# One bank and one evacuation for both heads of chunk 1, and the diagonal's sums in two blocks of 64 tokens

## The chip, the cores and the metric

The kernel runs on one core of one Trainium2 chip. The metric is the device time of one execution, in microseconds; lower is better. The kernel before takes 498.93 us (median of three runs, 497.51 to 500.3).

## The reference

The computation is a linear recurrence with a decaying state per batch and head, followed by a feed-forward layer with a PReLU between its two products. There are 4 batches, 8 heads, 768 tokens and 48 numbers per head; the layer goes from 384 to 2048 and back.

```python
for t in range(S):
    cur = np.einsum('bhd,bhe->bhde', u[None] * kt, vt)
    y[:, :, t] = np.einsum('bhd,bhde->bhe', rt, state + cur)
    state = w[None, :, :, None] * state + np.einsum('bhd,bhe->bhde', kt, vt)
...
h = x @ w_in                       # x: y as (3072, 384)
g = np.maximum(h, 0.0) + alpha * np.minimum(h, 0.0)
return (g @ w_out).astype(np.float32)
```

All of it is in fp32. The layer's products are made from pairs of fp32r numbers, a high part and the remainder: each product is hi*hi + lo*hi + hi*lo, three matmuls.

## The kernel before

**Chunks, pairs, steps.** The 768 tokens are cut into 6 chunks of 128, and the 8 heads into 4 pairs q. A pair keeps one head (g = 0) on partitions 0 to 47 and the other (g = 1) on partitions 64 to 111. The recurrence is done by chunk in matrix form: scores within the chunk (r times k, masked), the same token's own term on the diagonal (u), and the state carried from chunk to chunk. From chunk 1 on, a chunk is worked as two halves of 64 tokens (j = 0, 1).

The layer is worked in steps (c, i): chunk c and the i-th of 16 blocks of w_in and w_out. `m_in` (L628) makes a 128 x 512 block of h out of nine matmuls, ACT and DVE turn it into the pair gh, gl (L636 to L641), and `m_out` (L661) adds nine more to three accumulators. Steps 0 to 8 belong to chunk 0, steps 9 to 17 to chunk 1, and only then come the other 7 blocks for both chunks. For each block, its raw weights are loaded (L308, two buffers) and split by two operations on ACT and four on DVE (L326 to L337); the four have means of 0.55, 1.05, 1.00 and 0.98 us, 3.6 us of DVE a block; this must be done for blocks 0 to 8 in steps 0 to 8.

**Diagonal.** For chunks 0 and 1, `diagonal` (L466) gets the diagonal from TensorE: DVE multiplies r by k (`prod`, L468), four fp32 matmuls (one per batch, L473) multiply it by u/w (`uw`, 2 columns), and ACT copies the sums to `cu` (L477). An fp32 matmul leaves two records in the trace, so a diagonal has 8. `first_chunk` (L389) calls it once per pair, `prepare` (L485) once per pair of chunk 1. Later chunks take it from POOL.

**Chunk 0.** `first_chunk` scales r and k (L399), makes the diagonal, the scores (L410), the masked score matrix `base` (L417 on ACT, L421 on DVE), multiplies it by v (L431), and splits the result y into xh and xl with `splits` (L354): a copy on ACT (L361) and a subtraction on DVE (L362). For three pairs one operation each of 112 partitions x 512 does both heads; for the last pair there is one of 48 x 512 for each head.

**Later chunks.** `burst` (L524) does on PE the output of a pair whose `prepare` is done (`before`) and the products of the next one (`now`). The output of the pair `before` is summed in two banks, y[0] and y[1]: `through_state` (16 matmuls, L569), `through_scores(0)` (8, L579), and, after ACT has read two numbers of y[1] (`seen_y`, L592), `through_scores(1)` (8, L579). All these matmuls use a quarter of the array: rows 0 to 63 or 64 to 127 and columns 0 to 63 or 64 to 127. `where` puts head g into bank y[g], its batches 0 and 1 on its own half of the partitions and 2 and 3 on the other half:

```python
o = g ^ (b >> 1)
return y[g]()[half(o), (b & 1) * L + j * HI:(b & 1) * L + (j + 1) * HI]
```

Through the state, head g multiplies from rows half(g); so in each bank only one half of the array's rows writes at a time, and all four quarters are used. The products of the pair `now` (L543, L550) are laid out in the same way, in banks A[0] and A[1]; DVE takes them up with L598 and L605. The evacuation of a pair is four `splits` of 48 x 256 (two per head).

**Where the heads go.** Pair 0 goes to tiles of its own (`top`); pair q > 0 goes to block k = q - 1 of x. The rows 48 to 63 and 112 to 127 of that block are filled by `lower` (L344) with pieces of pair 0, by DMAs of 32 KB on SP's queue (L350). Parts 0 and 1 of a block are these rows, parts 2 to 5 the heads' rows. The first `m_in` of a chunk needs all of its x.

**The order.** Nothing is ordered by the hardware alone: `Plan.in_order` simulates the engines with the cost that each `add` states and a rank, and so writes the order of every engine's instructions, SP's queue among them. Five PSUM banks are handed out by it one at a time (`psum()`), to whoever is next: a diagonal's sums in chunk 1, y, A and the blocks of h. A burst takes its banks when it starts. Before the first step, gaps of the plan on PE are filled with small matmuls (`warm`, L721, counted by `fill`).

Of the kernel before, what the change touches and what calls it, by code (L numbers as in the profile page):

```python
# [18 lines left out]
L = 128  # L19
# [4 lines left out]
HI = 64  # L24
# [152 lines left out]
def rwkv_prelu_kernel(ctx: ExitStack, tc, rk, vkr, wP, uP, u, wall, alpha, w, r_all, k_all, v_all, oT):  # L177
# [288 lines left out]
    def diagonal(q, r, k0, cu, sums, cols, mine, prod_rank, sum_rank, copy_rank):  # L466
        prod = sb([112, B, L], "g", 3)
        add("DVE", 0.7, lambda: nc.vector.tensor_tensor(out=prod(), in0=r(), in1=k0(), op=ALU.mult),  # L468
            r=[r, k0], w=[prod], rank=prod_rank)

        def c_sum():
            for b in range(B):
                nc.tensor.matmul(sums()[:, cols][:, 2 * b:2 * b + 2], prod()[:, b], uw()[:, q], start=True,  # L473
                                 stop=True, skip_group_check=True)

        add("PE", 1.0, c_sum, r=[prod, uw], w=[mine], rank=sum_rank)
        add("ACT", 0.2, lambda: nc.scalar.activation(  # L477
            cu(), sums()[:, cols].rearrange("p (b g) -> p g b", g=2), AF.Copy), r=[mine], w=[cu], rank=copy_rank)
# [45 lines left out]
    def burst(i, was, at):  # L524
# [28 lines left out]
        if before:  # L553
            (c0, q0), r0, v0, base0, *states0 = before
            y = [psum() for _ in range(2)]
            uses += [r0, v0, base0, *states0]
            spare = psum()
            writes += y

            def where(g, b, j):  # L560
                o = g ^ (b >> 1)
                return y[g]()[half(o), (b & 1) * L + j * HI:(b & 1) * L + (j + 1) * HI]

            def through_state():
                for j, t in enumerate(states0):
                    for e in range(2):
                        for g in range(2):
                            for b in (e, e + 2):
                                nc.tensor.matmul(where(g, b, j), t()[half(g), b],  # L569
                                                 r0()[half(g), b, HI * j:HI * (j + 1)], start=(j == 0 and e == 0),  # L570
                                                 stop=False, skip_group_check=True)
# [18 lines left out]
        if before:  # L590

            seen = add("ACT", 0.2, lambda: nc.scalar.activation(seen_y(), y[1]()[0:1, L + HI - 1:L + HI + 1], AF.Copy),  # L592
                       r=[y[1]], rank=at - 200)
            seen.soon[first] = 0.75
            add("PE", 0.3, lambda: through_scores(1), r=[v0, base0], w=y, rank=at - 200)
        if now:
# [13 lines left out]
        if before:  # L610
            h, l, kx = x_tiles(c0, q0)
            for g in (1, 0):
                for o in (g, 1 - g):
# [286 lines left out]
```

## Time and profile before

| what | us |
|---|---|
| median of three runs | 498.93 |
| the profiled execution, device time | 498.5 |
| its span, first to last instruction | 496.7 |
| PE busy (x4563) | 477.7 |
| DVE busy (x550) | 322.1 |
| ACT busy (x565) | 242.5 |
| mean granted TensorE clock | 0.987 |

A busy TensorE (PE) means that matmul records cover the time. The share of each engine over the whole span is an average over two stages that differ, so the views below are by stretch.

### The profile page before, as it was taken

Reading aid. Unit: us, or ns where it says so; the run is one execution under the profiler, and the core shown is the slowest. Engines: PE = TensorE matmul, PEld = TensorE weight load, DVE = VectorE, ACT = ScalarE, POOL = GpSimd, SP = SyncE. Lnnn points to the kernel's source line nnn. Section 1 sums busy time; section 2 is a strip of 40 time slices with the busy share of each in tenths; the row PEclk is TensorE's granted clock in tenths of the full one; section 3 lists DMA queues with packets and bytes.
Section 4 is the critical chain, followed back from the end, with each engine's and each line's share of the span. In section 5 each row is a group of like instructions: output and inputs, shape, how many; then the busy total and the mean of one; then the engine's idle time right before and its main releaser. Section 6 shows DMA issues by size and latency. Waiting matters only on the chain.

```text
span 496.7 us, 11103 instructions
## 1 busy us (share of the span) xinstructions
PE 477.7 (96%) x4563; PEld 390.2 (79%) x4563; DVE 322.1 (65%) x550; ACT 242.5 (49%) x565; POOL 45.1 (9%) x49
## 2 busy tenths in 40 slices
PE   7989878999999999999999999999999999999994
PEld 6857756788888888888888888888888878888883
DVE  7799999999986677656647546747535434333331
ACT  3777557666764455535535635535633333423332
POOL 2000100001312112100311101211000000000000
PEclk9799999999999999999999999999999999999998
DMA  7965575374152253413212213312120000100001
GB/s 220 299 172 189 153 226 196 126 233 161 49 189 90 80 169 100 147 43 83 86 36 86 95 56 84 86 36 70 63 54 1 1 1 1 64 0 2 0 1 68
DMA packets 24888, 47.39 MB, mean 95 GB/s; under 512 B 4096, under 2 KB 12416, under 8 KB 24832
## 3 DMA queue, kind: packets, MB, share of 16 engines
q1 hardware_dynamic: 24832, 46.62, 30.3%
q8 instruction: 38, 0.62, 0.5%
q14 instruction: 18, 0.15, 0.1%
HBM read 37.96 MB, written 6.29 MB: 89 GB/s over the span
## 4 chain that ended last, share of the span: by engine, by line
PE 84%; DVE 8%; ACT 3%; DMA 2%; issue 1%; SPq 0%; DVEq 0%; ACTq 0%
PE acc L661 38%; PE bank L628 36%; PE bank L569 2%; PE bank L579 2%; PE bank L550 2%; PE bank L543 2%; DMA wraw<-wall 1%; DVE wx L333 1%; DVE xl L362 1%; DMA raw<-rk 1%; DVE wl L337 1%; DVE wx L330 1%; DVE g L637 1%; PE acc L473 1%; DVE raw L496 1%
## 5 line engine op out<-in xcount | busy, mean ns | idle before, releaser
L637 DVE SCALAR_TENSOR_TENSOR g<-bank,alph,g 128x512 f32<-128x512 f32 x96 | 72.0, 750 | 110.0 <-ACT g L636 108.5
L636 ACT ACTIVATE g<-bank 128x512 f32<-128x512 f32 x96 | 57.3, 597 | 141.0 <-PE bank L628 139.1
L628 PE MATMUL bank<-xh,wh 128*128 128x512 f32 x288 | 113.6, 395 | 3.4 <-DVE T L605 3.4
L628 PE MATMUL bank<-xh,wl 128*128 128x512 f32 x288 | 112.3, 390 | 0.4 <-DVE wl L337 0.3
L628 PE MATMUL bank<-xl,wh 128*128 128x512 f32 x288 | 112.1, 389 | 0.0
L640 ACT ACTIVATE gh<-g 128x512 fp32r<-128x512 f32 x96 | 60.6, 632 | 71.3 <-DVE g L637 71.1
L641 DVE TENSOR_TENSOR gl<-g,gh 128x512 fp32r<-128x512 f32 x96 | 70.0, 730 | 37.1 <-ACT gh L640 37.0
L661 PE MATMUL acc<-gh,wh 128*128 128x512 f32 x288 | 83.6, 397 | 1.6 <-ACT gh L640 1.6
L661 PE MATMUL acc<-gl,wh 128*128 128x512 f32 x288 | 83.2, 396 | 0.0
L661 PE MATMUL acc<-gh,wl 128*128 128x512 f32 x288 | 81.7, 391 | 0.0
L628 PEld LDWEIGHTS bank<-xh,wh 128*128 128x128 f32 x288 | 54.1, 188 | 15.8 <-ACT wx L326 3.8
L628 PEld LDWEIGHTS bank<-xh,wl 128*128 128x128 f32 x288 | 54.1, 188 | 12.6 <-DVE wl L337 1.3
L661 PEld LDWEIGHTS acc<-gl,wh 128*128 128x128 f32 x288 | 54.1, 188 | 12.1
L628 PEld LDWEIGHTS bank<-xl,wh 128*128 128x128 f32 x288 | 54.0, 188 | 11.7
L661 PEld LDWEIGHTS acc<-gh,wl 128*128 128x128 f32 x288 | 53.9, 188 | 11.6
L661 PEld LDWEIGHTS acc<-gh,wh 128*128 128x128 f32 x288 | 52.6, 188 | 13.2 <-ACT gh L640 1.9
L507 POOL TENSOR_TENSOR rr<-rr,kk 128x384 f32<-128x384 f32 x16 | 21.4, 1337 | 294.9 <-DMA kk<-vkr 155.8
L518 ACT ACTIVATE base<-ident,cu 128x64 f32<-128x64 f32 x160 | 41.4, 337 | 1.1 <-DVE cu L513 1.0
L362 DVE TENSOR_TENSOR xl<-bank,xh 48x256 fp32r<-48x256 f32 (+2 forms) x85 | 37.2, 438 | 3.5 <-ACT xh L361 1.7
L361 ACT ACTIVATE xh<-bank 48x256 fp32r<-48x256 f32 (+2 forms) x85 | 33.3, 392 | 7.8 <-PE bank L431 3.4
L496 DVE TENSOR_TENSOR raw<-raw,W 112x512 f32<-112x512 f32 x40 | 26.3, 681 | 0.3 <-DMA raw<-rk 0.3
L509 POOL TENSOR_TENSOR rr<-rr,utab 128x384 f32<-128x384 f32 x16 | 21.0, 1310 | 1.3
(93 smaller groups left out, 375.1 us busy)
## 6 DMA issues: line engine op xcount, KB each, us to landing
wraw<-wall SPq DMA_DIRECT2D x16, 768.0 KB, 4.8
raw<-rk SPq DMA_DIRECT2D x46, 224.0 KB, 4.2
v<-vkr SPq DMA_DIRECT2D x24, 192.0 KB, 4.0
kk<-vkr SPq DMA_DIRECT2D x24, 192.0 KB, 3.6
rr<-vkr SPq DMA_DIRECT2D x16, 192.0 KB, 2.4
oT<-o SPq DMA_DIRECT2D x12, 256.0 KB, 2.1
oT<-g SPq DMA_DIRECT2D x6, 256.0 KB, 2.6
xh<-xh SPq DMA_DIRECT2D x36, 32.0 KB, 2.5
```

The lines of the kernel that those rows point to most:

```text
L361: add("ACT", us, lambda: nc.scalar.activation(to(h), view(), AF.Copy), r=[src], w=refs(h), rank=rank)
L362: add("DVE", us + 0.1, lambda: nc.vector.tensor_tensor(out=to(l), in0=view(), in1=to(h), op=ALU.subtract), r=[src] + refs(h), w=refs(l), r ...
L496: add("DVE", 0.72, lambda t=t, tab=tab: nc.vector.tensor_tensor(out=t().rearrange("p b (j t) -> p (b j) t", j=2), in0=t().rearrange("p b ( ...
L507: add("POOL", 1.2, lambda: nc.gpsimd.tensor_tensor(out=rt(), in0=rt(), in1=k(), op=ALU.mult), r=[k] + ([wh[12]] if c == 2 else []), w=[rt] ...
L509: add("POOL", 1.2, lambda: nc.gpsimd.tensor_tensor(out=rt().rearrange("p (g b) e -> p g b e", g=2), in0=rt().rearrange("p (g b) e -> p g b ...
L518: add("ACT", 0.32, lambda g=g, b=b: nc.scalar.activation(base()[:, g, b], ident2(), AF.Copy, scale=cu()[:, g, b:b + 1]), r=[cu, ident2], w ...
L628: nc.tensor.matmul(hp()[:, :], a[i]()[:, k], x[c]()[:, k], start=(k == 0 and j == 0), stop=(k == NK - 1 and j == 2))
L636: add("ACT", 0.6, lambda: nc.scalar.activation(g(), hp()[:, :], AF.Copy), r=[hp], w=[g], rank=n - 100)
L637: add("DVE", 0.75, lambda: nc.vector.scalar_tensor_tensor(out=g(), in0=hp()[:, :], scalar=alph()[:, i:i + 1], in1=g(), op0=ALU.mult, op1=A ...
L640: add("ACT", 0.64, lambda: nc.scalar.activation(gh(), g(), AF.Copy), r=[g], w=[gh], rank=n - 100)
L641: add("DVE", 0.73, lambda: nc.vector.tensor_tensor(out=gl(), in0=g(), in1=gh(), op=ALU.subtract), r=[g, gh], w=[gl], rank=n - 99)
L661: nc.tensor.matmul(banks[k](), a[i]()[:, NK + k], x(), start=(begin and j == 0), stop=(end and j == 2))
```

## The change

The change has two parts. In `diagonal`, each of the four matmuls becomes two, of 64 tokens each, whose results go to partitions 0 to 63 and 64 to 127; the planner's cost of the piece goes from 1.0 to 0.5. In `burst`, when the pair `before` is of chunk 1 (`joint`), both heads' outputs go to one bank: head g on its own half of the partitions, batch b at column 128 b. Then the evacuation is one operation of 112 x 512 per engine for pairs 0 to 2, which also writes part 0 of the block (rows 48 to 63), and one of 48 x 512 per head for pair 3. A bank is taken from the planner for one y in place of two. `spare` was not used by any piece.

```diff
--- before.py
+++ after.py
@@ -470,10 +470,12 @@
 
         def c_sum():
             for b in range(B):
-                nc.tensor.matmul(sums()[:, cols][:, 2 * b:2 * b + 2], prod()[:, b], uw()[:, q], start=True,
-                                 stop=True, skip_group_check=True)
-
-        add("PE", 1.0, c_sum, r=[prod, uw], w=[mine], rank=sum_rank)
+                for j in range(2):
+                    s = slice(HI * j, HI * (j + 1))
+                    nc.tensor.matmul(sums()[s, cols][:, 2 * b:2 * b + 2], prod()[:, b, s], uw()[:, q], start=True,
+                                     stop=True, skip_group_check=True)
+
+        add("PE", 0.5, c_sum, r=[prod, uw], w=[mine], rank=sum_rank)
         add("ACT", 0.2, lambda: nc.scalar.activation(
             cu(), sums()[:, cols].rearrange("p (b g) -> p g b", g=2), AF.Copy), r=[mine], w=[cu], rank=copy_rank)
 
@@ -552,12 +554,14 @@
                                              skip_group_check=True)
         if before:
             (c0, q0), r0, v0, base0, *states0 = before
-            y = [psum() for _ in range(2)]
+            joint = c0 == 1
+            y = [psum()] * 2 if joint else [psum() for _ in range(2)]
             uses += [r0, v0, base0, *states0]
-            spare = psum()
-            writes += y
+            writes += y[joint:]
 
             def where(g, b, j):
+                if joint:
+                    return y[g]()[half(g), b * L + j * HI:b * L + (j + 1) * HI]
                 o = g ^ (b >> 1)
                 return y[g]()[half(o), (b & 1) * L + j * HI:(b & 1) * L + (j + 1) * HI]
 
@@ -567,7 +571,7 @@
                         for g in range(2):
                             for b in (e, e + 2):
                                 nc.tensor.matmul(where(g, b, j), t()[half(g), b],
-                                                 r0()[half(g), b, HI * j:HI * (j + 1)], start=(j == 0 and e == 0),
+                                                 r0()[half(g), b, HI * j:HI * (j + 1)], start=(j == 0 and b in (0, 0 if joint else 2)),
                                                  stop=False, skip_group_check=True)
 
             def through_scores(crossed):
@@ -589,10 +593,11 @@
         first = add("PE", (0.7 if before else 0.1) + (0.8 if now else 0.1), run, r=uses, w=writes, rank=at)
         if before:
 
-            seen = add("ACT", 0.2, lambda: nc.scalar.activation(seen_y(), y[1]()[0:1, L + HI - 1:L + HI + 1], AF.Copy),
-                       r=[y[1]], rank=at - 200)
+            row, col = (HI, L) if joint else (0, L)
+            seen = add("ACT", 0.2, lambda: nc.scalar.activation(
+                seen_y(), y[1]()[row:row + 1, col + HI - 1:col + HI + 1], AF.Copy), r=[y[1]], rank=at - 200)
             seen.soon[first] = 0.75
-            add("PE", 0.3, lambda: through_scores(1), r=[v0, base0], w=y, rank=at - 200)
+            add("PE", 0.3, lambda: through_scores(1), r=[v0, base0], w=y[joint:], rank=at - 200)
         if now:
             for g in range(2):
                 add("DVE", 0.42, lambda g=g: nc.vector.copy_predicated(
@@ -609,7 +614,13 @@
             made[i] = now, r, v, base, T0, T1
         if before:
             h, l, kx = x_tiles(c0, q0)
-            for g in (1, 0):
+            if joint and q0 < P - 1:
+                splits(kx, h, l, y[0], lambda: y[0]()[0:112, :], slice(0, 112), slice(0, NT), [0, 2, 3, 4, 5], 0.6, at - 0.3)
+            elif joint:
+                for g in range(2):
+                    splits(kx, h, l, y[g], lambda g=g: y[g]()[half(g), :], half(g), slice(0, NT),
+                           [2 + 2 * g, 3 + 2 * g], 0.6, at - 0.3)
+            for g in () if joint else (1, 0):
                 for o in (g, 1 - g):
                     n0 = 0 if o == g else 2 * L
                     splits(kx, h, l, y[g], lambda g=g, o=o: y[g]()[half(o), 0:2 * L], half(g),
```

## Rows read from the trace of the kernel before

**Rows 1.** The page, busy time, share of the span and instructions of each engine.

```profile
PE 477.7 (96%) x4563; PEld 390.2 (79%) x4563; DVE 322.1 (65%) x550; ACT 242.5 (49%) x565; POOL 45.1 (9%) x49
```

**Rows 2.** Busy time of each engine in stretches of the span (us from its start). Columns: the stretch and its length, then for PE, PEld, DVE, ACT and POOL the busy us and (x instructions), the granted TensorE clock as a share of full speed, the DMA share and GB/s.

```profile
8.70:13.00 4.30, 4.29 (x48) 3.93 (x48) 4.30 (x8) 3.10 (x12) 0.00 (x0) 0.95 1.07 299
13.00:19.80 6.80, 6.80 (x58) 6.54 (x56) 3.83 (x14) 4.33 (x15) 0.00 (x0) 0.53 1.02 320
19.80:31.20 11.40, 10.95 (x127) 8.58 (x122) 11.07 (x19) 10.41 (x31) 0.00 (x0) 1.00 0.57 154
31.20:91.50 60.30, 51.21 (x737) 39.94 (x734) 59.08 (x99) 39.06 (x93) 2.92 (x2) 0.97 0.67 209
91.50:490.00 398.50, 398.50 (x3573) 327.03 (x3571) 238.78 (x402) 183.48 (x415) 39.42 (x30) 1.00 0.22 68
```

**Rows 3.** The chain of work that ended last, in order of time, from 8.7 to 19 us (start, us, what).

```profile
8.71 1.02 PE acc L473 x8
...
10.82 0.98 PE acc L473 x8
11.81 1.27 PE acc L410 x16
13.08 1.79 PE acc L473 x8
14.87 2.01 PE bank L410 x16
16.88 1.93 PE bank L431 x14
...
18.83 0.60 ACT xh L361
```

**Rows 4.** Timeline of DVE in the same stretch (start, us, engine, line, operation, and in brackets the idle time before it with what ended it).

```profile
11.35 0.63 DVE L468 TENSOR_TENSOR g<-raw 112x512 f32<-112x512 f32 x1
...
16.98 0.73 DVE L421 COPY_PREDICATED base<-strict,bank 128x512 f32<-128x512 uint8 x1 [1.19 <-PE bank L410]
19.46 0.69 DVE L362 TENSOR_TENSOR xl<-bank,xh 112x512 fp32r<-112x512 f32 x1 [1.75 <-ACT xh L361]
```

**Rows 5.** Timeline of ACT in the same stretch.

```profile
18.83 0.60 ACT L361 ACTIVATE xh<-bank 112x512 fp32r<-112x512 f32 x1 [2.44 <-PE bank L431]
```

**Rows 6.** The chain of work that ended last, in order of time, from 63 to 95 us.

```profile
63.38 0.42 PE bank L579 x14
...
63.82 0.44 DVE base L598
...
89.53 0.88 DVE wl L337
...
90.45 4.17 PE bank L628 x17
```

**Rows 7.** Groups of instructions of the whole span, with shapes kept apart: line, engine, operation, out<-in, shapes, count | busy us, mean ns of one | idle before.

```profile
L362 DVE TENSOR_TENSOR xl<-bank,xh 48x256 fp32r<-48x256 f32 x80 | 33.8, 422 | 1.7
L361 ACT ACTIVATE xh<-bank 48x256 fp32r<-48x256 f32 x80 | 30.4, 380 | 4.4 <-PE bank L579 3.1
...
L457 PE MATMUL bank<-v,kk 128*64 128x48 f32 x32 | 2.6, 225 | 1.7 <-issue 1.7
...
L457 PE MATMUL bank<-v,kk 128*48 128x48 f32 x32 | 2.2, 212 | 0.0
...
L362 DVE TENSOR_TENSOR xl<-bank,xh 112x512 fp32r<-112x512 f32 x3 | 2.1, 686 | 1.7 <-ACT xh L361 1.7
...
L361 ACT ACTIVATE xh<-bank 112x512 fp32r<-112x512 f32 x3 | 1.8, 589 | 2.4 <-PE bank L431 2.4
...
L362 DVE TENSOR_TENSOR xl<-bank,xh 48x512 fp32r<-48x512 f32 x2 | 1.4, 689 | 0.0
```

**Rows 8.** Timeline of PE at seven places (weights rows*columns, then out<-in partitions x elements; a group that alternates between two forms is shown under one).

```profile
21.29 1.16 PE L410 MATMUL acc<-o 48*128 48x128 f32 x16
22.38 1.05 PE L473 MATMUL acc<-uw,g 112*128 112x2 f32 x8
...
37.88 1.05 PE L473 MATMUL bank<-uw,g 112*128 112x2 f32 x8
38.79 0.48 PE L628 MATMUL bank<-xh,wh 128*128 128x512 f32 x1
...
47.01 0.67 PE L457 MATMUL bank<-v,kk 128*64 128x48 f32 x16
47.60 0.50 PE L628 MATMUL bank<-xh,wh 128*128 128x512 f32 x1
...
50.59 0.67 PE L569 MATMUL bank<-raw,T 48*48 48x64 f32 x32
51.07 0.41 PE L579 MATMUL bank<-base,v 64*48 64x64 f32 x16
51.30 0.57 PE L543 MATMUL bank<-v,kk 64*64 64x48 f32 x30
```

**Rows 9.** Who waited for whom on PE from 30 to 100 us (total us, times, longest).

```profile
PE bank L628 <- DVE T L605: 3.4, 1, 3.4
```

**Rows 10.** Timeline of SP's DMA issues.

```profile
67.08 0.42 SPq L308 DMA_DIRECT2D wraw<-wall  x1
...
70.39 3.68 SPq L350 DMA_DIRECT2D xl<-xl  x6
```

## The prediction

> **What bounds the kernel now.** I read the engines' totals first. PE covers 96% of the span and DVE 65% [rows 1], which says only that PE is the engine to look at. The table by stretch then splits the run in two [rows 2]. From 91.5 us to 490.0 us PE is busy for all of 398.5 us: there the kernel lasts as long as its matmuls. From 31.2 to 91.5 us it is otherwise: DVE is busy for 59.1 of 60.3 us and PE for 51.2, so PE idles 9.1 us. So the end moves one for one with the moment at which PE stops waiting, at about 91 us. The chain of waits says the same: it runs over DVE, with PE between (63.38, then DVE at 63.82), and passes to PE for good at 90.45, after the last low half of a weight block at 89.53 [rows 6]. What is taken from DVE, or from a wait of DVE, before 91 us is worth its full length; what is taken from PE there is worth little until its 9.1 us of idle time are used up.
>
> Before 19.8 us the chain is different: it alternates on PE between the diagonal's sums (L473) and the scores (L410), ends with the first pair's output (L431) at 16.88, and passes to ACT at 18.83 [rows 3]. DVE waits there for the scores (1.19) and for ACT's copy (1.75), and ACT for L431 (2.44) [rows 4, 5]. From 13.0 to 19.8 us the granted clock is 0.53, the lower level of 1.2 GHz, and L410 takes 2.01 there against 1.27 at 11.81 [rows 2, 3].
>
> **Part 1, the diagonal's sums.** Eight records of 128 tokens become sixteen of 64, in two column halves of the array. One diagonal now takes 38.79 - 37.88 = 0.91 us [rows 8]. The trace has no matmul of 64 by 2. The nearest is L457, all 128 rows, alternating between a tile of 64 columns and one of 48 (the two forms in rows 7): 16 records in 47.60 - 47.01 = 0.59 us [rows 8]. That is my value, a saving of 0.32 at full clock and, at the ratio 0.59/0.91, 0.63 where it took 1.79 [rows 3]. At worst the halves run one after the other (below).
>
> On the early path, one step at a time: the first sums end at 8.71 + 0.59 = 9.30, plus 1.09 for scores = 10.39. The second pair of scores then starts at 10.98 in place of 11.81 and ends near 12.25. The third product is ready at 11.35 + 0.63 = 11.98 [rows 4], so the sums run to about 12.9, and the scores, still slow, to 14.9 in place of 16.88. L431 starts 2.0 us early, and so does ACT's copy, for ACT had 2.44 of idle time. DVE gets up to 2.0 us of its 2.94 back. I take 1.5, not 2.0: the planner now counts 0.5 per piece, may reorder PE, and fills its gaps with small matmuls. The ends are 0 and 2.4, all of ACT's idle time. DVE is busy 11.07 of 11.40 from 19.8 to 31.2, so a lead at its start is not eaten by idle time later [rows 2].
>
> The four diagonals of chunk 1 save 4 x 0.32 = 1.3 on PE, in a stretch where PE idles: no gain by itself.
>
> The Trainium skill, page "TensorE: Matmul & The Clock Gate", section "Part 3: Packing small matmuls — row/col tiling", speaks against this part: there a weight load overlaps running matmuls only when its row group differs, and the two blocks share all rows. By it the sums would stay near 0.9 and the early 1.5 would be nothing; L457, where two column tiles with the same rows do 16 records in 0.59, is against it.
>
> **Part 2, the evacuation.** On DVE 16 operations of 422 ns go (6.75 us), and three of 686 and two of 689 come (3.44): -3.3 [rows 7]. On ACT 16 of 380 ns (6.1) give way to five of 0.59 (2.9): -3.1, with the one-head copy taken like the one of 112 rows [rows 7]. ACT is busy 39 of 60 us, so this costs and gives nothing by itself [rows 2]. All four pairs are done in the DVE-bound stretch, so -3.3 is taken whole. Ends: -3.0, if the last pair's share (4 x 0.42 - 2 x 0.69 = 0.3) comes after the handover, and -3.3.
>
> **Part 2, the matmuls.** Head g now always uses quarter (g, g) of the array in L569 and the first L579, and the two crossed quarters in the second: two quarters where there were four. A tile's pace: with four tiles L569 does 32 records of 64 columns in 51.07 - 50.59 = 0.48, 8 a tile, 0.06 each; with two tiles L410 does 16 records of 128 columns in 22.38 - 21.29 = 1.09, 8 a tile, 0.14 each [rows 8]. So a tile needs its own time per column however many work beside it, and half the tiles mean twice the time: +0.48 for L569 and +0.23 (51.30 - 51.07) for each L579, 0.94 a pair, 3.8 for four. Less the 1.3 above this is +2.5 on PE, under 9.1 of idle time. What cover there is not: DVE's L598 takes up the products the moment PE ends (63.38 + 0.42, then 63.82) [rows 6], and the products now start 0.71 later in the burst; the static order keeps DVE waiting. It meets three bursts and the last evacuation. I take two of four, 1.4; the ends are 0 and 4 x 0.71 = 2.8.
>
> **Edits that I cost at nothing.** One bank less per burst: PE's longest idle, 3.42 us, is L628 waiting for L605 to free a bank [rows 9]; a spare bank may let it start, but DVE is what is late next. The one added wait: rows 48 to 63 of blocks 0 and 1 are now overwritten by the joint copy, so four of the small DMAs come after it. Behind them on SP's queue stand loads of weights and of chunk 2 (67.08, 70.39) [rows 10]. Pair 1 was evacuated at about 70 anyway, so I expect the planner to put the loads first; if not, a weight block is some 3 us late (70.39 - 67.08).
>
> **Sum:** -1.5 - 3.3 + 1.4 = -3.4 on a profiled execution of 498.5, so 495.1. That one stands 0.4 below the median of 498.93, which gives **495.5**.
>
> **The rivals.** A measurement of this kernel can tell about 0.5% from no change, 2.5 us: faster is below 496.4, slower above 501.4.
>
> *The gain is swallowed (498.5).* The order of all engines is written anew from other costs. If a weight load is 3 us late behind the small DMAs, DVE stands still for about what it saved. For it: SP's queue is in order. Against: DVE's order has other work in almost every gap. -3.4 + 3 = -0.4.
>
> *The blocks do not run side by side (497.3).* The sums take 16 x 0.07 = 1.1 (0.59 over the 8 records of one 64-column tile). Then the early path gains nothing or loses some 0.3, and -3.3 + 1.4 + 0.3 = -1.6 is left. Against it: L457.
>
> *Two halves of the rows cannot write one bank at once (503).* Before, L569, L579, L543 and L550 never let both halves of the array's rows write one bank in the same stretch; now both do, in y. If they take turns, 32 records at 0.06 are 1.92 in place of 0.48 and each L579 0.96 in place of 0.23: +2.9 a pair, 11.6 for four, 10.3 after the sums. PE becomes the bound from the point where the extra work exceeds its usable idle time, which I put at half of 9.1: 10.3 - 4.5 = +5.8, less 1.5 early, +4.3. Against it: the partitions are disjoint, and nothing shows a penalty for them; for it, no row of before has the case. The Trainium skill, page "TensorEngine Tiling (Array Packing)", section "Gotcha 1: PSUM Pressure", says that different row tiles cannot access one bank simultaneously and that software must see to it; it gives no price, and no run here shows it yet.
>
> **How the numbers follow.** Forecast 0.55, its own range 492.5 to 497.5: 0.46 faster, 0.09 same. Swallowed 0.20: 0.02, 0.16, 0.02. Blocks in turn 0.13: 0.05, 0.07, 0.01. Bank in turn 0.12: 0, 0.01, 0.11. Sums: faster 0.53, same 0.33, slower 0.14. The low end is both gains at their best, no delay in the bursts and the low clock stretch partly left: -2.4 - 3.3 = -5.7, then 1.5 of the 1.8 us that L410 and L431 lose there (2.01 + 1.93 against twice the 1.09 of L410 at full clock) [rows 3, 8]: 491.7. The high end, 500.5, leaves out most of the bank case.
>
> **What would show it.** Right: a diagonal's 16 records in about 0.6; L431 near 15 us and ACT's copy near 17; five operations in place of 16 in L361 and L362; L569 of chunk 1 near 0.96 for 32 records and still 0.48 later; PE free of idle time from about 88 us; no more PE idle after that. Wrong: sums at 0.9 or more (part 1), L569 near 1.9 (bank), DVE with new idle time before 88 us that ends on a DMA or on PE (swallowed, or my 1.4 too small), or the handover to PE still at 91.

## The result, and the profile after

The changed kernel takes 502.57 us (median of 22 runs, 499.12 to 506.38) against 500.31 us for the kernel before beside it (22 runs): the ratio is 1.0053, with a 95% interval of 1.0032 to 1.0074. It is some 2.3 to 2.7 us slower. The forecast was 3.4 us faster; the time lies outside the range and on the other side. Ratios leave out runs more than 1.5% above the fastest of the same kernel: at most one in most experiments, but 3 of 7 in p1_order, 4 of 12 in after_poolq and 3 of 12 in costs_pool2, where the median of all runs is given beside the ratio.

The profiled execution took 503.42 us, 0.9 above its median, and the one of before 1.8 below its own. So of the 4.9 us between the two traces about half belongs to the change; no difference of 2 us between two traces is read below without the timed runs.

The page's engine totals, in the columns of [rows 1]:

```profile
PE 478.5 (95%) x4637; PEld 389.6 (78%) x4637; DVE 319.2 (64%) x539; ACT 238.8 (48%) x554; POOL 43.2 (9%) x49
```

PE's busy time grew by 0.8, its idle time from 496.7 - 477.7 = 19.0 to 501.6 - 478.5 = 23.1 us. The time went into waits of PE. The table by stretch, in the columns of [rows 2], shows where:

```profile
13.00:19.80 6.80, 6.01 (x81) 4.56 (x79) 6.25 (x18) 5.31 (x18) 0.00 (x0) 1.00 1.06 278
...
31.20:91.50 60.30, 48.86 (x718) 38.21 (x718) 53.61 (x85) 31.66 (x74) 2.38 (x2) 0.95 0.64 198
91.50:96.50 5.00, 3.77 (x14) 2.77 (x13) 3.58 (x6) 2.65 (x4) 0.00 (x0) 0.89 0.46 157
96.50:490.00 393.50, 393.50 (x3552) 323.24 (x3552) 235.00 (x395) 181.25 (x411) 38.15 (x30) 1.00 0.22 69
```

From 13.0 to 19.8 us the granted clock is 1.00 for 0.53, but that is this execution: after_pool2 and after_warm, which issue the same work in the same order up to there, have 0.61 and 0.59. From 31.2 to 91.5 DVE is busy 5.5 us less than before, and ACT 7.4 less. And yet PE is also busy less, and it is saturated only after 91.5, where it idles another 1.23 us. DVE has less to do, as forecast, and PE did not get the time.

**What came as forecast.** The timeline of PE at the first diagonal, the first output and the first joint output through the state (compare [rows 8] and [rows 3]):

```profile
8.91 0.63 PE L475 MATMUL acc<-uw,g 112*64 112x2 f32 x16 [0.83 <-DVE g L468]
9.47 0.71 PE L410 MATMUL bank<-raw 48*128 48x128 f32 x8
...
13.75 0.96 PE L431 MATMUL bank<-base,v 128*64 128x128 f32 x14
...
51.52 1.13 PE L573 MATMUL bank<-raw,T 48*48 48x64 f32 x32 [0.73 <-DVE T L610]
52.45 0.55 PE L583 MATMUL bank<-base,v 64*48 64x64 f32 x13
```

Sixteen half sums take 9.47 - 8.91 = 0.56 us (0.59 was forecast, 0.91 before). L431 starts at 13.75 in place of 16.88, at the higher clock. The joint L573 takes 52.45 - 51.52 = 0.93 for 32 records (0.96 forecast), with the two halves of the rows writing one bank.

The groups by form, in the columns of [rows 7]:

```profile
L362 DVE TENSOR_TENSOR xl<-bank,xh 112x512 fp32r<-112x512 f32 x6 | 4.1, 684 | 0.0
...
L362 DVE TENSOR_TENSOR xl<-bank,xh 48x512 fp32r<-48x512 f32 x4 | 2.8, 689 | 1.5 <-ACT xh L361 1.4
```

Three more of 112 rows and two more of 48, at the prices that the prediction took.

**Where the early lead ends.** DVE's timeline at the first and the last subtraction of chunk 0 and at the first layer step, in the kernel after:

```profile
16.90 0.68 DVE L362 TENSOR_TENSOR xl<-bank,xh 112x512 fp32r<-112x512 f32 x1
...
29.98 1.39 DVE L362 TENSOR_TENSOR xl<-bank,xh 48x512 fp32r<-48x512 f32 x2 [0.17 <-ACT xh L361]
...
35.67 0.56 DVE L328 TENSOR_SCALAR wx<-wx 128x768 uint32<-128x768 uint32 x1 [1.24 <-ACT wx L326]
...
38.59 0.75 DVE L648 SCALAR_TENSOR_TENSOR g<-bank,alph,g 128x512 f32<-128x512 f32 x1 [1.22 <-ACT g L647]
```

and the last two of them in the kernel before:

```profile
31.56 1.39 DVE L362 TENSOR_TENSOR xl<-bank,xh 48x512 fp32r<-48x512 f32 x2
...
37.86 0.75 DVE L637 SCALAR_TENSOR_TENSOR g<-bank,alph,g 128x512 f32<-128x512 f32 x1
```

The lead is 19.46 - 16.90 = 2.6 us at the first subtraction and 1.58 at the last. How much of it is the change's own cannot be told from these two traces, for the last subtraction also starts earlier where the granted clock of 13.0 to 19.8 us was higher. DVE in before_poolq (the sums and the order of the kernel before; clock 0.75), and in after_pool2 (those of the changed kernel; 0.61):

```profile
29.71 1.39 DVE L362 TENSOR_TENSOR xl<-bank,xh 48x512 fp32r<-48x512 f32 x2
```

```profile
31.12 1.39 DVE L362 TENSOR_TENSOR xl<-bank,xh 48x512 fp32r<-48x512 f32 x2 [0.30 <-ACT xh L361]
```

With the early work of before, executions start the last subtraction at 29.71, 31.56 (clock 0.53) and 32.81 (p2_old_order, 0.50); with that of the changed kernel at 29.98 (1.00), 31.12 and 31.46 (after_warm, 0.59).

Whatever the lead, some eight microseconds later it is a lag of 0.73. In between DVE idles, and PE waits. The chain of waits (start, us, what) in that stretch, after, says for what, and PE's timeline shows the wait:

```profile
30.11 4.77 DMA xh<-xh
```

```profile
35.02 0.76 PE L639 MATMUL bank<-xh,wh 128*128 128x512 f32 x1 [3.60 <-DMA xh<-xh]
```

It is one of the last 32 KB DMAs that fill chunk 0's x. SP's timeline, after and then before, shows it 0.6 us behind a 768 KB load of weights, in both kernels:

```profile
29.50 0.51 SPq L308 DMA_DIRECT2D wraw<-wall  x1
30.11 0.51 SPq L350 DMA_DIRECT2D xh<-xh  x1
```

```profile
29.27 0.58 SPq L308 DMA_DIRECT2D wraw<-wall  x1
29.95 0.51 SPq L350 DMA_DIRECT2D xh<-xh  x1
```

In the kernel before, DVE came to the subtraction at 31.56 and had work without a pause until the step (no row of DVE there names idle time). The DMA took 4.6 us there and landed at 34.6, and PE went on with the step just after:

```profile
35.08 0.50 PE L628 MATMUL bank<-xh,wh 128*128 128x512 f32 x1
```

So the DMA was hidden, but by half a microsecond only. In the changed kernel everything else is ready earlier, and the first layer step waits for the DMA, 3.60 us on PE: it goes on at 35.02, no earlier than before. The lead bought nothing but the wait. The table of both kernels for 31.2 to 36 us, before and then after:

```profile
31.20:36.00 4.80, 3.09 (x43) 2.37 (x40) 4.73 (x8) 2.62 (x5) 0.00 (x0) 1.00 0.93 313
```

```profile
31.20:36.00 4.80, 1.20 (x3) 0.83 (x3) 3.53 (x6) 1.25 (x2) 0.00 (x0) 0.86 0.94 329
```

**Where PE waits later.** It waits for the weight block for step 8. The chain of waits from 77 to 97 us:

```profile
77.22 0.96 DVE wx L333
...
78.23 7.53 DMA wraw<-wall
...
85.84 0.90 ACT wx L326
87.47 0.53 ACT gh L651
...
88.04 0.97 PE acc L672 x3
...
96.25 3.88 PE bank L639 x17
```

A raw buffer comes free when DVE's L333 has read it; SP then loads the block after next; ACT splits it (L326, L336), and behind that split in ACT's order stands `gh` of a layer step, for which PE waits. PE waits 3.22 us before 88.04 and, behind the next block's split, 1.23 before 95.28. In [rows 6] PE took over for good at 90.45; here at 96. What stood around that load on SP's queue, after, and then before (a pair's inputs of chunk 2 are r and k0 in `raw`, then v and kk):

```profile
73.70 2.23 SPq L375 DMA_DIRECT2D raw<-rk  x2
...
78.23 0.33 SPq L308 DMA_DIRECT2D wraw<-wall  x1
```

```profile
76.11 0.33 SPq L308 DMA_DIRECT2D wraw<-wall  x1
76.49 1.29 SPq L375 DMA_DIRECT2D raw<-rk  x2
```

In the kernel before, the weight load goes first, and the loads of a pair of chunk 2 follow it; in the changed one they go first, and the weight load takes 7.53 us, for 4.3 before. It also starts 2.1 us later (78.23 for 76.11), as L333 frees its buffer later. Nothing in the diff moves a load. The planner wrote the queue anew from the new costs and bank counts.

PE's timeline there also shows what a wait leaves behind:

```profile
88.04 0.97 PE L672 MATMUL acc<-gh,wh 128*128 128x512 f32 x3 [3.22 <-ACT gh L651]
88.84 0.39 PE L639 MATMUL bank<-xh,wh 128*128 128x512 f32 x1
...
89.36 0.63 PE L639 MATMUL bank<-xl,wh 128*128 128x512 f32 x1
...
95.28 0.97 PE L672 MATMUL acc<-gh,wh 128*128 128x512 f32 x3 [1.23 <-ACT gh L651]
```

After 3.22 us of idle time the granted clock falls, and a matmul that took 0.39 takes 0.63, until 92.3. The table above has 0.89 for 91.5 to 96.5.

### The profile page after: what moved, and what is told of

It is laid out like the page before. It is cut to its first block, busy times and chain, and to the rows that moved or that the text cites. A ratio compares the mean times of both kernels' runs of the same rounds, so it can differ in the third digit from the quotient of the medians.

```text
span 501.6 us, 11225 instructions
## 1 busy us (share of the span) xinstructions
PE 478.5 (95%) x4637; PEld 389.6 (78%) x4637; DVE 319.2 (64%) x539; ACT 238.8 (48%) x554; POOL 43.2 (9%) x49
## 4 chain that ended last, share of the span: by engine, by line
PE 84%; DVE 6%; DMA 5%; ACT 2%; issue 1%; SPq 1%; ACTq 0%; DVEq 0%
PE bank L639 38%; PE acc L672 38%; DMA wraw<-wall 3%; PE bank L573 3%; PE bank L583 2%; PE bank L552 2%; PE bank L545 1%; DMA o<-rk 1%; DVE wx L333 1%; DMA xh<-xh 1%; ACT wx L326 1%; DVE wx L330 1%; SPq L375 1%; DVE raw L498 1%; DVE g L648 1%
## 5 line engine op out<-in xcount | busy, mean ns | idle before, releaser
L639 PE MATMUL bank<-xh,wh 128*128 128x512 f32 x288 | 114.8, 399 | 5.8 <-DMA xh<-xh 3.6
L639 PE MATMUL bank<-xl,wh 128*128 128x512 f32 x288 | 113.3, 394 | 0.0
L362 DVE TENSOR_TENSOR xl<-bank,xh 48x256 fp32r<-48x256 f32 (+2 forms) x74 | 33.9, 458 | 2.8 <-ACT xh L361 1.4
L361 ACT ACTIVATE xh<-bank 48x256 fp32r<-48x256 f32 (+2 forms) x74 | 30.1, 407 | 4.4 <-PE bank L583 1.9
L511 POOL TENSOR_TENSOR rr<-rr,utab 128x384 f32<-128x384 f32 x16 | 19.9, 1242 | 1.3
```

Of the source, the lines that this page charges most:

```text
L361: add("ACT", us, lambda: nc.scalar.activation(to(h), view(), AF.Copy), r=[src], w=refs(h), rank=rank)
L362: add("DVE", us + 0.1, lambda: nc.vector.tensor_tensor(out=to(l), in0=view(), in1=to(h), op=ALU.subtract), r=[src] + refs(h), w=refs(l), r ...
L511: add("POOL", 1.2, lambda: nc.gpsimd.tensor_tensor(out=rt().rearrange("p (g b) e -> p g b e", g=2), in0=rt().rearrange("p (g b) e -> p g b ...
L639: nc.tensor.matmul(hp()[:, :], a[i]()[:, k], x[c]()[:, k], start=(k == 0 and j == 0), stop=(k == NK - 1 and j == 2))
```

## The experiments

Theory A: the work of both parts is as cheap as forecast or neutral, and the loss comes from the order that the planner wrote anew and the DMAs that are late in it. Rivals: one of the parts costs time by itself (PE's longer bursts, the split sums); DVE bounds the stretch, so that the loss must be found on it; or the lower clock after PE's waits takes the time. Every ratio is to the kernel before, timed beside it, with its 95% interval.

### The parts, with and without the new order

**p1_order.** The kernel before with the planner told 0.5 for a diagonal's sums, the matmuls unchanged.

```diff
-        add("PE", 1.0, c_sum, r=[prod, uw], w=[mine], rank=sum_rank)
+        add("PE", 0.5, c_sum, r=[prod, uw], w=[mine], rank=sum_rank)
```

> Only the planner's cost of the diagonal's sums goes from 1.0 to 0.5; the matmuls are those of before. So every engine gets the order that part 1 alone brings, with the work of before. Theory A (the new order of the queues loses the time): slower than before by 1 to 4 us. Theory B (the work itself loses it, the outputs on half of the array's quarters above all): within 1 us of before.

Measured: 1.0024 (0.9974 to 1.0075), from 4 of only 7 runs; the median of all 7, 504.22, is 1.0084 times that of before. Inconclusive by itself.

**p1_alone.** Part 1 of the diff as it is; part 2 left out.

```diff
+                for j in range(2):
+                    s = slice(HI * j, HI * (j + 1))
+                    nc.tensor.matmul(sums()[s, cols][:, 2 * b:2 * b + 2], prod()[:, b, s], uw()[:, q], ...
-        add("PE", 1.0, c_sum, ...)
+        add("PE", 0.5, c_sum, ...)
```

> Part 1 as in the change, chunk 1's outputs as before. The order is that of the run with the planner's cost alone; what differs is the sums in two blocks, 0.57 in place of 0.91 us each. A: within 1 us of that run, for the first weight block's load ends near 19.8 us and swallows what the sums give early. B: 1 to 2 us faster than before, since the order costs nothing and the sums give their early 1.5.

Measured: 1.0030 (1.0006 to 1.0054), 501.58 us. Slower by about 1.5 us, with all of part 1's work saved.

**p1_work.** The same split sums, but the planner is still told 1.0 (the edit is shown against p1_alone). Every engine's order stays that of the kernel before.

```diff
-        add("PE", 0.5, c_sum, ...)
+        add("PE", 1.0, c_sum, ...)
```

> Part 1's matmuls (two blocks of 64 tokens) in the order of before: the planner still counts 1.0. A (the order loses the time, the work doesn't): 0 to 1.5 us faster than before, less than the early 2 us, since the first weight block's load ends late. B (part 1's shorter work itself hurts, by the idle time it leaves on PE): slower than before, as the run with part 1 alone was, by 1 us or more.

Measured: 1.0010 (0.9979 to 1.0040). The sums by themselves neither cost nor give anything that can be told. In its trace PE waits 3.5 us at the first layer steps for ACT's split (L326) of a weight block, whose load was issued at 28.77, behind four small DMAs, and took 5.40: in the old order too, a transfer is what is late next.

**p2_alone.** Part 2 as it is; part 1 left out (sums whole, told 1.0).

```diff
-        add("PE", 0.5, c_sum, ...)      # and the loop over j
+        add("PE", 1.0, c_sum, ...)
```

> Part 2 as in the change, the sums as before. A: anywhere from 2 us faster to 4 us slower, by where the new order puts the loads of weight blocks; its sign follows the landing of the block for step 8. B: slower by 2 to 4 us, four times the 0.94 us of longer matmuls, with the PE's idle time no longer on loads but on the outputs.

Measured: 0.9993 (0.9964 to 1.0021). No change, although its order is new too: not every new order loses.

**both_old_order** and **p2_old_order.** The joint bank in the order of the kernel before: the planner still sees two banks and four evacuations a pair, of which two are empty and two are of 48 x 512. Of the four operations of 0.42 us a pair, two of 0.69 are left: 4 x (1.69 - 1.38) = 1.2 us less DVE work, not 3.3. The first also has the split sums.

```diff
+            one = [y[0], y[0]] if joint else y
...
+                    if joint:
+                        splits(kx, h, l, y[g], lambda g=g: y[0]()[half(g), :], half(g), slice(0, NT),
+                               [2 + 2 * g + (o != g)], 0.38, at - 0.3, idle=o != g)
+                        continue
```

> Both parts' work in the order of before: the planner is told the old costs, the old banks and the old pieces; the sums run in two blocks, y goes to one bank, and of the four evacuations of a pair two are done (48 x 512 for each head) and two are left empty. The one operation of 112 rows isn't in it, since in the old order the DMAs to rows 48 to 63 come first. A: faster than before by 0.5 to 2.5 us (DVE gives 16 x 0.42 - 8 x 0.69 = 1.2). B: slower by 1 to 3 us, as the matmuls on half the quarters are all in it.

> Part 2's work alone in the order of before: y in one bank, two evacuations of 48 x 512 per engine and pair and two left empty, the sums as before. A: within 1 us of before or a little faster (DVE gives 1.2 and more, the matmuls take 0.9 a pair of PE's idle time). D (the two-quarter matmuls cost their full length): slower by 2 to 4 us.

Measured: 0.9980 (0.9958 to 1.0003) and 1.0008 (0.9980 to 1.0037). With the order held, the new work costs nothing that can be told: against 1.0053, both parts in the old order are 3.6 us faster, with less of DVE's saving in them than the change has. This is the strongest case for theory A, and it speaks against a loss by PE's longer bursts or by the bank, which are both in it.

### Is DVE the bound?

**before_less_dve.** The kernel before, with 7.6 us of chunk 1's DVE operations empty and the order unchanged.

```diff
-            add("DVE", 0.72, lambda t=t, tab=tab: nc.vector.tensor_tensor(
+            add("DVE", 0.72, lambda t=t, tab=tab: hasty or nc.vector.tensor_tensor(
...
-        add("DVE", 0.56, lambda: scale_k(k, whalf, q), r=[whalf], w=[k], rank=at - 1.6)
+        add("DVE", 0.56, lambda: hasty or scale_k(k, whalf, q), r=[whalf], w=[k], rank=at - 1.6)
```

> The kernel before, its order kept, without the scaling of r, k and the second k of chunk 1's pairs (L496 and L382 for chunk 1, in place, so these numbers stay unscaled): 8 x 0.68 + 4 x 0.55 = 7.6 us less on DVE between 24 and 84 us, none of it on the path of the weight blocks. If DVE's total is what sets the handover at 91 us, as the prediction had it: 5 to 7.6 us faster. If the chain that one weight block hands to the next (load, ACT, DVE, load of the block after next) and the fixed order set it: under 2 us.

Measured: 0.9982 (0.9957 to 1.0007), so 0.9 us of 7.6, and not told from nothing. The table by stretch:

```profile
31.20:91.50 60.30, 52.12 (x742) 41.45 (x739) 51.56 (x83) 36.92 (x90) 2.60 (x2) 0.89 0.60 191
```

DVE has 8.7 us of idle time where it had 1.2, and PE still idles 8.2. The chain of waits of this kernel at one place shows what paces it with DVE relieved:

```profile
63.97 0.88 DVE wx L333
...
64.91 4.34 DMA wraw<-wall
...
69.34 0.90 ACT wx L326
...
70.28 6.54 PE bank L628 x15
```

It is the loop of a raw weight buffer: DVE reads it out, the load of the block after next follows (4.34 us), then ACT's split, and in the written order PE comes behind that. The chain of the kernel before, ahead of the part in [rows 6], has the same loop with a load of 6.64 us:

```profile
48.61 0.88 DVE wx L333
...
49.54 6.64 DMA wraw<-wall
...
56.29 0.04 ACT wx L326
```

In these places DVE's work is not what the end waits for, however busy DVE is meanwhile.

**costs_less_dve.** The same work left out of the kernel after_costs below.

> The changed kernel planned with the measured PE costs, with the same 7.6 us of DVE work left out for chunk 1's pairs as before (r, k and the product's k are not scaled, so the output differs). The order is the same in all other respects. In the old order this left the time almost as it was (0.9982). Theory A, DVE's total is not the bound in this order either: ratio 0.994 to 0.998. Rival B, once the weight blocks come early, DVE is the bound after all: 2 to 6 us less, ratio 0.984 to 0.992.

Measured: 0.9941 (0.9909 to 0.9972), against 0.9957 for after_costs: 0.8 us of 7.6, within the intervals. DVE's total is not the bound in that order either.

### The two late DMAs

**after_w8_first.** The changed kernel; the loads of chunk 2's pairs 1 and 2 are kept behind the load of the block for step 8.

```diff
+        late = [raws[8]] if c == 2 and q in (1, 2) else []
...
-                t().rearrange("p b t -> p (b t)"), rk[c, q, :, j * NT:(j + 1) * NT]), 224, early + 0.1 * q + 0.01 * j)
+                t().rearrange("p b t -> p (b t)"), rk[c, q, :, j * NT:(j + 1) * NT]), 224, early + 0.1 * q + 0.01 * j, late)
...
```

> The changed kernel, with the loads of chunk 2's pairs 1 and 2 kept behind the load of the weight block for step 8. A: that block lands some 3 us earlier than 85.8, PE's 3.2 us wait before step 7's outputs shrinks to under 1, and the kernel is 1.5 to 3 us faster than the changed kernel, 500 to 501. C (what costs is the clock that falls after PE's idle stretches, the one at 31 to 35 us first): within 1 us of the changed kernel.

Measured: 0.9997 (0.9969 to 1.0026). About 2.8 us of the changed kernel's time come back. PE's waits for `gh` fall from 4.5 to 1.6 us; the wait on the small DMA is still there:

```profile
PE bank L640 <- DMA xh<-xh: 3.8, 1, 3.8
...
PE acc L673 <- ACT gh L652: 1.6, 2, 1.3
```

**after_two.** That, and the load of the block for step 2 kept behind chunk 0's last small DMAs.

```diff
-        raw = raws.get(i) or raw_weights(i, need - 9)
+        raw = raws.get(i) or raw_weights(i, need - 9, [(xh[0], (1, 0)), (xl[0], (1, 0))] if i == 2 else ())
```

> As the changed kernel with the block for step 8 ahead of chunk 2's loads, and the load of the block for step 2 kept behind chunk 0's last small DMAs, which PE waits for until 35.0. A: PE's first wait falls from 3.8 to about 1.3 us, step 0 is 1 to 2.5 us earlier, the block for step 2 is 1 us later; time within 1.5 us of that kernel (500.4), better rather than worse. C (the early low clock stretch matters): 1.5 us faster or more.

Measured: 0.9950 (0.9918 to 0.9982), 498.51 us: faster than before. In its trace the wait on the small DMA is 0.3 us. Both edits make the planner write the order anew, so they are no clean removal of one wait; the next one is.

**after_pool2.** The changed kernel, with only the load of block 2 issued from POOL's queue. The order of PE, DVE and ACT is exactly that of the changed kernel.

```diff
-        load(t, lambda: nc.sync.dma_start(t().rearrange("p f a -> p (f a)"), ...
+        load(t, lambda: (nc.gpsimd if i == 2 else nc.sync).dma_start(t().rearrange("p f a -> p (f a)"), ...
```

> The changed kernel itself, with only the load of weight block 2 issued from POOL's queue; the order of PE, DVE and ACT is that of the changed kernel. Theory A, the wait of 3.6 us of PE at 35 us goes and 1.5 to 3 us of it reach the end: ratio to the kernel before 0.999 to 1.0025. Rival B, in this order the later waits (3.2 and 1.2 us on ACT at 88 and 95 us) take the gain up: ratio 1.0035 to 1.007.

Measured: 0.9991 (0.9963 to 1.0020), 500.20 us. One DMA on another queue gives back about 3.1 us of the changed kernel's time. There it is also issued earlier, at 25.8 in place of 29.50, so the run does not tell the queue from the time of issue. PE's timeline at the first layer steps:

```profile
33.49 0.39 PE L639 MATMUL bank<-xl,wh 128*128 128x512 f32 x1
35.90 0.49 PE L639 MATMUL bank<-xh,wh 128*128 128x512 f32 x1 [2.03 <-ACT wh L336]
```

The first step's nine matmuls run without a pause; the second step waits for its own weights instead, and what follows is 1.7 us earlier than in the changed kernel, although chunk 0's last subtraction was 1.1 us later (31.12):

```profile
36.94 0.75 DVE L648 SCALAR_TENSOR_TENSOR g<-bank,alph,g 128x512 f32<-128x512 f32 x1
```

**after_poolq** and **before_poolq.** The loads of blocks 2 to 8 on POOL's queue (`2 <= i <= 8`), in the changed kernel and in the kernel before.

> The changed kernel, with the loads of weight blocks 2 to 8 issued from POOL's queue in place of SP's. The order of PE, DVE and ACT is exactly that of the changed kernel. Theory A, the changed kernel loses its time to loads that stand in the wrong place of SP's queue: the load for step 8 starts when its buffer is free, the small DMAs of chunk 0 no longer stand behind the load for step 2, and the time falls by 2 to 4 us against the changed kernel, ratio to the kernel before 0.995 to 1.001. Rival B, the order of PE, DVE and ACT itself is the loss: the time stays that of the changed kernel, ratio 1.003 to 1.007.

> The kernel before, with the loads of weight blocks 2 to 8 issued from POOL's queue in place of SP's. The order of PE, DVE and ACT stays as it was. Theory A, the place of a weight load in SP's in-order queue is part of what sets the handover in the old order too: these loads no longer wait for SP's earlier entries, and the time falls by 0.5 to 2 us, ratio 0.996 to 0.999. Rival B, the loads are limited by the release of their two buffers and by the traffic itself, not by their place in the queue: no change, 0.998 to 1.002. Rival C, with the loads out of its way SP starts the small DMAs and the loads of chunk 2 earlier, and they take traffic from the weights: slower, 1.002 or more.

Measured: after_poolq 0.9960 (0.9929 to 0.9991), but over 8 of its 12 runs; the median of all 12, 501.04 us, is 1.0018 times that of before. It points the same way as after_pool2 and proves no more. Its load of block 8 was issued at 74.95 and still needed 7.8 us: with loads of chunk 2 under way its place in SP's queue is not what makes it long; the shared traffic may be. before_poolq 1.0025 (0.9998 to 1.0053): no gain. It is the edit of after_poolq, and it holds the move of block 2's load that gave the changed kernel 3.1 us; in the kernel before, the small DMA behind the weights was hidden, so taking the load out of its way is worth nothing. That fits what the two traces show at 31 to 36 us.

### The clock

**after_warm.** The changed kernel, with 24 small matmuls in the first layer step, to keep PE busy while it waits.

```diff
+                if n == 0 and k == 0:
+                    for _ in range(24):
+                        warm()
```

> The changed kernel, with 24 small matmuls (2.6 us) on PE after the first three of step 0, where PE waits 3.6 us for a DMA; nothing else moves. C: the low clock stretch at 34.6 us is gone, step 0 ends 1.3 us earlier, and the kernel is 1 to 2 us faster than the changed kernel. A: step 0 may end earlier, but loads and DVE set the pace to 96 us: within 0.7 us of the changed kernel.

```profile
31.20:91.50 60.30, 52.31 (x778) 41.48 (x775) 56.95 (x89) 35.66 (x82) 2.20 (x2) 1.00 0.65 203
```

Measured: 1.0051 (1.0020 to 1.0083), median 502.91: the time of the changed kernel. The row, with a granted clock of 1.00, is of an execution of 499.38, 3.5 us under that median, so it does not say what the clock was in the others. What says more is the mean granted clock of every run: 0.986 on average here and 0.985 over the changed kernel's 22 runs, so the small matmuls hardly raised it; and 0.979 to 0.981 for the kernel before, in each of the five batches timed beside the experiments. The changed kernel is slower at the higher clock, so a lower clock is not where its time went. The faster orders below have a higher one still, 0.991 for after_costs and 0.996 for costs_poolq; what share of their gain goes with it is not shown.

### The planner's costs

**after_costs.** The changed kernel, with the planner told about what the joint matmuls take: the through-state and first scores 1.3 in place of 0.7, the crossed scores 0.6 in place of 0.3.

```diff
-        first = add("PE", (0.7 if before else 0.1) + (0.8 if now else 0.1), run, r=uses, w=writes, rank=at)
+        first = add("PE", (1.3 if before and joint else 0.7 if before else 0.1) + (0.8 if now else 0.1), run, r=uses, w=writes, rank=at)
...
-            seen.soon[first] = 0.75
-            add("PE", 0.3, lambda: through_scores(1), r=[v0, base0], w=y[joint:], rank=at - 200)
+            seen.soon[first] = 1.35 if joint else 0.75
+            add("PE", 0.6 if joint else 0.3, lambda: through_scores(1), r=[v0, base0], w=y[joint:], rank=at - 200)
```

> The changed kernel, with the planner told what chunk 1's outputs take on PE (1.3 in place of 0.7, 0.6 in place of 0.3, and 1.35 to the copy that the second half waits for); instructions as in the changed kernel, order by the new costs. If the planner's false costs are what makes its order bad: 1.5 to 3 us faster than the changed kernel. If the order is good or bad by chance of a tie between loads: anywhere within 3 us of it.

Measured: 0.9957 (0.9933 to 0.9982), 498.13 us. The same instructions in another order are 4.8 us faster than the changed kernel. PE's waits for `gh` are 0.5 us; the one on the small DMA (3.7) is left.

**w8_costs.** after_costs and after_w8_first together.

> Both at once: the block for step 8 ahead of chunk 2's loads, and the planner told the outputs' true costs. A: as the kernel with the loads mended alone, 500.4 within 1 us, or up to 2 us better if the outputs then meet less waiting.

Measured: 1.0000 (0.9974 to 1.0026), 500.48 us. That is where it was expected; but after_costs alone gave 0.9957, so two edits that each helped do not add up. Each makes the planner write another order, which is the likely reason, not a shown one. A new order moves this kernel by some 2 us, and not in a way that I could foresee.

**costs_pool2** and **costs_poolq.** after_costs with the load of block 2, or of blocks 2 to 8, on POOL's queue; the order of PE, DVE and ACT stays that of after_costs.

> The changed kernel planned with the measured PE costs, with only the load of weight block 2 issued from POOL's queue; the loads of blocks 3 to 8 stay on SP's. With all seven moved the ratio was 0.9893, with none 0.9957. Theory A, the one load that stands ahead of chunk 0's last small DMAs is what counts, and its wait of 3.7 us of PE at 35 us: ratio 0.988 to 0.993. Rival B, the gain came from the later loads, or from the luck of six runs: ratio 0.9945 to 0.998.

> The changed kernel planned with the measured PE costs, and the loads of weight blocks 2 to 8 issued from POOL's queue. Its order without that gave 0.9957; one wait of 3.7 us of PE on a small DMA behind the load for step 2 was left at about 35 us. Theory A: that wait goes and the time falls by another 0 to 2 us, ratio 0.992 to 0.996. Rival B: the wait goes but nothing comes of it, ratio 0.9955 to 0.998.

Measured: 0.9938 (0.9908 to 0.9967) and 0.9893 (0.9856 to 0.9931; 494.88 us, only 6 runs). The first is from 9 of its 12 runs and lies between the two expectations; the median of all 12, 498.26, is 0.9960 times that of before, and it cannot be told from after_costs. The second is the fastest of all. The table by stretch and the page of the second:

```profile
PE 476.5 (97%) x4637; PEld 387.3 (79%) x4637; DVE 319.6 (65%) x539; ACT 239.0 (48%) x554; POOL 49.0 (10%) x56
```

```profile
31.20:91.50 60.30, 55.47 (x751) 42.35 (x751) 57.93 (x95) 35.27 (x80) 5.89 (x8) 1.00 0.66 199
```

In a span of 493.2 PE idles 16.7 us, for 23.1 in the changed kernel, and it does 55.5 us of work from 31.2 to 91.5 for 48.9, at a clock of 1.00 for 0.95. DVE is busy 4.3 us *more* there than in the changed kernel, and yet PE waits less.

## Why the prediction was wrong

**The step that failed** is the first: "What is taken from DVE, or from a wait of DVE, before 91 us is worth its full length", and with it "-3.3 is taken whole". The 59.1 of 60.3 us in [rows 2] were read as a bound. Taking 7.6 us from DVE in the unchanged order moved the end by 0.9, not 7.6 (before_less_dve). At the places shown, one of them in the kernel before, at 49.54, and so ahead of where [rows 6] begins, the loop of the raw weight buffers (L333, load, L326) paces the stretch, and the chain of [rows 6] shows only which engine's instruction came last at each handover. That chain even passed "the last low half of a weight block at 89.53"; I took it as DVE work, not as the end of a loop that begins with a DMA.

**The early 1.5** was lost, whatever its size. In the traced execution DVE starts chunk 0's last subtraction 1.58 us early, but that this meets the forecast is luck: the execution kept the higher clock, and with the sums and the order of before the start moves by 3.1 us between executions (29.71 to 32.81). I argued that DVE was too busy for the lead to be eaten by idle time, and looked at DVE alone; what is late next is a DMA on SP's queue that had been hidden, and it turns the lead into a lag of 0.73. Part 1 alone in the old order gives 1.0010; moving the one load gives 3.1 us.

**The -3.3 on DVE's own time** was sized right (six and four operations at 684 and 689 ns), and **the longer matmuls** too (0.93 for L573), but their price of 1.4 on the end cannot be seen: in the old order both parts together lose nothing.

**The order written anew**, to which I gave a price only in a rival, was the largest term: 3.6 us between both_old_order and the changed kernel. That rival, "gain swallowed", had the right place (SP's queue, weight loads and small DMAs, 3 us) with the roles exchanged: the small DMA stands behind the weight load, as it did before, and not the load behind the small DMAs. It was priced once, and set against a gain of 3.3 that did not exist; the loads of chunk 2 ahead of block 8's are a second place, worth about 2.8 (after_w8_first). I also saw that a matmul of two quarters takes twice as long, and did not ask what the planner, still told 0.7 and 0.3, would do with that. Told 1.3 and 0.6, it wrote an order 4.8 us faster.

**The other rivals** are out. The blocks do run side by side: sixteen records took 0.56, where in turn they would have taken 1.1 by the prediction's rows. The Trainium skill, page "TensorE: Matmul & The Clock Gate", section "Part 3: Packing small matmuls — row/col tiling", lets a weight load overlap running matmuls only when its row group differs; read as the prediction read it, that would have left the sums near 0.9, and the trace, with 0.56, does not agree. And two halves of the rows may write one bank at once: 32 records took 0.93, twice the 0.48 of four tiles, which the two tiles explain alone, where a turn-taking would have been 1.92. The Trainium skill, page "TensorEngine Tiling (Array Packing)", section "Gotcha 1: PSUM Pressure", says that different row tiles cannot access one bank simultaneously; the 0.93 here does not agree.

**What stays open.** In the old order neither 7.6 us less DVE work nor the weight loads on another queue gave anything that can be told; the two were not tried together, and the loop that holds it there was shown at two places only. A third raw buffer, which would loosen the loop, was not tried. Why after_costs and after_w8_first do not add up is not settled, and neither is how much of the faster orders' gain goes with their higher clock.

## What to carry to other kernels

When a planner writes the order from stated costs, an edit changes two things, the work and the order. Time them apart: keep the old order with the new work (a cost left as it was, an empty piece), and give the new one the measured costs before you judge the change. And an engine that is 98% busy in a stretch is a bound only if taking work from it moves the end; before counting on that, look for the transfer that is hidden behind it now and would be late next.

## What was not expected of the hardware

A 32 KB DMA issued 0.6 us behind a 768 KB load on the same queue took 4.77 us to land, where the median of such DMAs from 24 to 36 us is 2.3. A 768 KB load with a pair's inputs of chunk 2 under way took 7.53 us, and still 7.8 from POOL's queue (after_poolq); in the kernel before, with those inputs issued behind it, 4.3. Two row halves of the array wrote one bank in disjoint partitions at their full pace (0.93 us for 32 records, 0.06 us a tile and record), and column halves with the same rows ran side by side: 16 records in 0.56 us.
